# Prefetching transfers moved from SyncE's queue to ScalarE's, and parts of the next chunk's preparation moved forward, in a fused mLSTM and FFN kernel

## The chip, the cores and the metric

The kernel runs on one core of one Trainium2 chip. The metric is device time in microseconds (us); the runs of one kernel lay 0.15 to 1.4% apart. The compute engines are TensorE (PE; PEld is its weight load), VectorE (DVE), ScalarE (ACT) and GpSimd (POOL). SyncE (SP) only issues transfers in this kernel. "SPq" and "ACTq" are the transfers issued from SyncE's and ScalarE's instruction streams.

## The reference

Two blocks follow each other: an mLSTM cell over 4 batches, 8 heads, 768 steps and head size 40, then a squared-ReLU FFN from 320 to 2048 and back on the 3072 tokens.

```python
for t in range(S):                                   # mLSTM, per batch and head
    m_new = maximum(f[t] + m, i[t])
    C = exp(f[t] + m - m_new) * C + exp(i[t] - m_new) * outer(v[t], k[t])
    n = exp(f[t] + m - m_new) * n + exp(i[t] - m_new) * k[t]
    y[t] = sigmoid(o_gate[t]) * (C @ q[t]) / maximum(abs(n @ q[t]), 1)
x = y, heads side by side                            # 3072 x 320
h = maximum(x @ w_in, 0)
return (h * h) @ w_out
```

## The kernel before

The steps are cut into 24 chunks of 128 steps; the attention is computed chunk by chunk, with a state C carried from one to the next. TensorE's attention work of a chunk stands between parts of the FFN of earlier chunks, so that TensorE always has something to do. The main loop has four FFN parts a chunk (`at` is 0 to 3) and starts with chunk 6.

Turning matrices is done without TensorE: data goes out to DRAM and comes back in a layout in which VectorE's 32x32 transposes finish the turn. So a chunk needs many small transfers: k and q out ("pair-ups", four, `kq_rows`) and in ("squares", four, `kqT`), the numerator out and back (`num_rows`), x out and back (`x_rows`, `xT`), and a broadcast of decay rows (`A_bc`). All of them are issued by SyncE, in program order.

```python
def pair_up(s):                      # four transfers, k and q of chunk s
    ...
            nc.sync.dma_start(kq_d[s, i, n]..., src[b, ...]...)

def load_squares(s):                 # four transfers
    ...
            nc.sync.dma_start(t[...], kq_d[s, i, ...]...)

def score(s):
    scores(s)                        # k q^T on TensorE
    weighted(s)                      # P = scores * W, on VectorE
    scale_q(s)                       # q's product: decay times turned q, on VectorE

for n, (which, g, i) in enumerate(parts):
    s, at = 6 + n // 4, n % 4
    ...
    if at == 0:
        do(score, s)
    if at == 1:
        do(attend_turned, s)         # numT = C q + V P on TensorE, then tn (a transpose) and the new C
        ...
    if at == 3:
        do(normalise_turned, s)      # x from num and the gate, on VectorE
        do(store_rows, s)            # x out and back, five transfers
        if s % 4 == 3:               # chunks 7, 11, 15, 19
            ... sigmoid(r) ...       # the gates of four later chunks, on ScalarE
    ... the FFN part: matmuls, ReLU on ScalarE, squares on VectorE, or the copy of m1 on ScalarE ...
    if at == 2:
        do(load_squares, s + 2)
        do(weigh_on, s + 1)          # W on ScalarE, then the broadcast load_A(s + 3)
        do(turn_kq, s + 1)
    if at == 3:
        do(decay_C, s + 1)
    ...
    if at == 1:
        do(move_num, s)              # num out and back, five transfers
        do(load, s + 4)
        do(pair_up, s + 3)
```

The second half of the FFN uses a Strassen-like scheme: the first product of a step is copied by ScalarE (`m1`, the row `y_sb<-h_ps` of the ACT timeline), and the copy has to be done before TensorE may reuse its PSUM bank.

## Time and profile before

| | before |
|---|---|
| time, median of 3 | 541.83 us (541.43 to 542.83) |
| span of the profiled run | 542.6 us |
| TensorE busy / idle | 525.0 / 17.6 us |
| mean granted TensorE clock | 0.987 |
| ScalarE busy | 193.5 us (36%) |
| median from issue to landing of x's store | 4.2 us |

The prediction shows the lines on TensorE. In the view of waits, a row names engine, tile and line, what released it, then total us, times, and longest:

```profile
ACT r_sb L647 <- PE h_ps L632: 151.9, 24, 10.4
...
ACT y_sb L740 <- PE h_ps L715: 66.8, 11, 7.5
...
ACT y_sb L735 <- PE h_ps L715: 54.7, 11, 10.6
```

ScalarE waits for TensorE.

### The profile page before, as it was taken

Reading aid. Unit: us, or ns where it says so; the run is one execution under the profiler, and the core shown is the slowest. Engines: PE = TensorE matmul, PEld = TensorE weight load, DVE = VectorE, ACT = ScalarE, POOL = GpSimd, SP = SyncE. Lnnn points to the kernel's source line nnn. Section 1 sums busy time; section 2 is a strip of 40 time slices with the busy share of each in tenths; the row PEclk is TensorE's granted clock in tenths of the full one; section 3 lists DMA queues with packets and bytes.
Section 4 is the critical chain, followed back from the end, with each engine's and each line's share of the span. In section 5 each row is a group of like instructions: output and inputs, shape, how many; then the busy total and the mean of one; then the engine's idle time right before and its main releaser. Section 6 shows DMA issues by size and latency. Waiting matters only on the chain.

```text
span 542.6 us, 10288 instructions
## 1 busy us (share of the span) xinstructions
PE 525.0 (97%) x3929; PEld 457.9 (84%) x3929; DVE 333.0 (61%) x620; ACT 193.5 (36%) x460; POOL 97.1 (18%) x110
## 2 busy tenths in 40 slices
PE   9989989997999989999999999999999999999997
PEld 4868878885788988888888898888898888898997
DVE  8488988866865664565575575465575485341631
ACT  3767576470531431522422533321433413101100
POOL 3355633321211320011210111000111010000000
PEclk9897999998999999999999999999999999999999
DMA  9988698847557747657657557568555241120000
GB/s 192 227 186 198 151 175 196 207 127 137 119 134 138 143 115 148 130 131 148 129 127 153 129 124 157 122 131 158 128 124 125 61 94 44 40 53 1 26 24 25
DMA packets 238353, 67.53 MB, mean 124 GB/s; under 512 B 185728, under 2 KB 232832, under 8 KB 238304
## 3 DMA queue, kind: packets, MB, share of 16 engines
q1 hardware_dynamic: 238208, 66.68, 57.5%
q8 instruction: 31, 0.51, 0.4%
q10 hardware_dynamic: 96, 0.20, 0.1%
q14 instruction: 18, 0.15, 0.1%
HBM read 54.56 MB, written 17.86 MB: 133 GB/s over the span
## 4 chain that ended last, share of the span: by engine, by line
PE 74%; DVE 10%; DMA 7%; SPq 4%; issue 2%; ACT 2%; POOL 0%; DVEq 0%; POOLq 0%; ACTq 0%
PE h_ps L621 26%; PE h_ps L715 25%; PE h_ps L632 7%; PE tp L422 3%; PE numT L512 3%; PE numT L505 3%; PE h_ps L661 3%; DMA x_rows<-x_sb 2%; DMA xT<-x_rows 2%; PE hp L458 1%; DVE g L654 1%; DMA num_rows<-tn 1%; SPq L308 1%; ACT W_sb L384 1%; DMA raw<-in_moe_w_out_dram 1%
## 5 line engine op out<-in xcount | busy, mean ns | idle before, releaser
L621 PE MATMUL h_ps<-xT,w_in 128*128 128x256 f32 x768 | 175.8, 384 | 3.8 <-DVE xT L597 2.8
L621 PEld LDWEIGHTS h_ps<-xT,w_in 128*128 128x128 f32 x768 | 143.7, 191 | 26.5 <-DVE xT L597 4.2
L647 ACT ACTIVATE r_sb<-h_ps 128x512 f32<-128x512 f32 x96 | 50.0, 601 | 155.0 <-PE h_ps L632 151.9
L654 DVE TENSOR_TENSOR g<-r_sb 128x512 f32<-128x512 f32 x96 | 61.7, 702 | 60.8 <-ACT r_sb L647 60.8
L715 PE MATMUL h_ps<-w_out,g 128*128 128x160 f32 x528 | 77.0, 302 | 0.0
L715 PEld LDWEIGHTS h_ps<-w_out,g 128*128 128x128 f32 x528 | 72.5, 190 | 1.4
L358 POOL TENSOR_SCALAR_AFFINE_SELECT A_bc<-A_bc 128x1024 f32<-128x1024 f32 x22 | 27.2, 1237 | 200.5 <-ACT kq L368 105.5
L384 ACT ACTIVATE W_sb<-A_bc,b_T 128x128 f32<-128x128 f32 x176 | 53.8, 391 | 24.3 <-POOL A_bc L358 24.2
L715 PE MATMUL h_ps<-T,S 128*128 128x160 f32 x352 | 52.3, 302 | 0.0
L715 PEld LDWEIGHTS h_ps<-T,S 128*128 128x128 f32 x352 | 48.8, 190 | 3.0 <-ACT r_sb L647 3.0
L632 PE MATMUL h_ps<-xT,w_in 64*128 64x256 f32 x384 | 49.0, 391 | 0.0
L632 PEld LDWEIGHTS h_ps<-xT,w_in 64*128 64x128 f32 x384 | 34.8, 186 | 12.3 <-issue 9.0
L597 DVE STREAM_TRANSPOSE xT<-xT 128x384 f32<-128x384 f32 x18 | 10.4, 576 | 46.3 <-DMA xT<-x_rows 46.3
L396 POOL TENSOR_TENSOR vw<-va,W_sb 128x328 f32<-128x328 f32 x20 | 20.1, 1003 | 86.6 <-ACT W_sb L384 74.9
L731 DVE TENSOR_TENSOR y_sb<-y_sb,h_ps 128x160 f32<-128x160 f32 x44 | 14.1, 320 | 33.8 <-PE h_ps L715 32.6
L435 DVE TENSOR_TENSOR P_sb<-tp,W_sb 128x512 f32<-128x512 f32 x46 | 29.5, 683 | 1.9 <-PE tp L422 1.9
L527 DVE STREAM_TRANSPOSE tn<-numT 128x512 f32<-128x512 f32 x18 | 12.9, 717 | 28.0 <-PE numT L512 28.0
L740 ACT COPY y_sb<-h_ps 128x160 f32<-128x160 f32 x11 | 3.2, 293 | 66.8 <-PE h_ps L715 66.8
L422 PEld LDWEIGHTS tp<-kqT 40*128 40x128 f32 x384 | 24.2, 187 | 3.3 <-issue 2.3
L422 PE MATMUL tp<-kqT 40*128 40x128 f32 x384 | 26.9, 279 | 0.0
L715 PE MATMUL h_ps<-T,g 128*128 128x160 f32 x176 | 25.7, 299 | 0.0
L715 PE MATMUL h_ps<-w_out,S 128*128 128x160 f32 x176 | 25.7, 299 | 0.0
(119 smaller groups left out, 626.6 us busy)
## 6 DMA issues: line engine op xcount, KB each, us to landing
A_bc<-a_rows SPq DMA_DIRECT2D x22, 512.0 KB, 5.0
raw<-in_moe_w_out_dram SPq DMA_DIRECT2D x16, 320.0 KB, 3.4
num_rows<-tn SPq DMA_DIRECT2D x18, 256.0 KB, 2.3
kq<-num_rows SPq DMA_DIRECT2D x72, 64.0 KB, 1.9
kqT<-kq_rows SPq DMA_DIRECT2D x34, 128.0 KB, 2.9
raw<-in_moe_w_in_dram SPq DMA_DIRECT2D x8, 512.0 KB, 4.8
kq<-in_k_dram SPq DMA_DIRECT2D x24, 160.0 KB, 3.4
va<-in_v_dram SPq DMA_DIRECT2D x24, 160.0 KB, 3.9
```

The source lines that it names most:

```text
L358: nc.gpsimd.affine_select(A[:], A[:], compare_op=ALU.is_ge, fill=-1e30, base=0, pattern=[[0, H], [1, P]], channel_multiplier=-1,)
L384: nc.scalar.activation(d["W"][:, i * n + h, :], A[i][:, h, :], AF.Exp, bias=b_T[:, b, c, i * n + h : i * n + h + 1],)
L396: nc.gpsimd.tensor_tensor(d["vw"][:], d["va"][:], d["W"][:, :, P - 1 : P].to_broadcast([P, H, D1]), op=ALU.mult,)
L422: nc.tensor.matmul(sc[i][:, j, :], lhsT=d["kT"][rows, j, :], rhs=d["qT"][rows, j, :], start=True, stop=True,)
L435: nc.vector.tensor_tensor(t, d["sc"][i], d["W"][:, heads, :], op=ALU.mult)
L505: nc.tensor.matmul(numT[halves[i], j, :], lhsT=C[live[i], j * D1 : j * D1 + DP], rhs=d["eA"][live[i], j, :], start=(j == 0), stop=False, s ...
L512: nc.tensor.matmul(numT[halves[i], j, :], lhsT=va_w[s % NKQ][:, h * D1 : h * D1 + DP], rhs=d["P"][h % 2][:, h // 2, :] if s < KQ_SQ else d ...
L621: nc.tensor.matmul(hs[i][:, n, :], lhsT=w_in[:, a, fb * P : (fb + 1) * P], rhs=xT[:, :, a, :], start=(n == 0 and a == 0), stop=False,)
L632: nc.tensor.matmul(hs[i][:, n, :], lhsT=w_in2[rows, 2 * pp + n, :], rhs=xT[rows, :, 2, :], start=False, stop=(n == 1),)
L647: nc.scalar.activation(rs[-1][:], h[:], AF.Relu)
L654: nc.vector.tensor_tensor(g4[:, :, i, :], r[:], r[:], op=ALU.mult)
L715: nc.tensor.matmul(to, lhsT=lhsT[:, p], rhs=rhs[:, p, :], start=(start and p == 0), stop=(p == NPAIR - 1), skip_group_check=True,)
```

## The change

Its intent: free SyncE for the transfers that the current chunk's result hangs on (num, x and the output), and have decays, mask, turn and q's product of the next chunk ready one or two FFN parts earlier.

```diff
-    def pair_up(s):
+    def pair_up(s, queue):
...
-                nc.sync.dma_start(
+                queue.dma_start(
... (the same in load_squares and load_A)
     def score(s):
         scores(s)
         weighted(s)
-        scale_q(s)
...
         if at == 1:
             do(attend_turned, s)
+            do(decays, s + 1)
+            do(mask, s + 1)
+            if n > 4:
+                do(turn_kq, s + 1)
+            do(decay_C, s + 1)
...
+        if at == 2:
+            do(lambda s: load_squares(s, nc.scalar), s + 2)
+            if n > 4:
+                do(scale_q, s + 1)
         if at == 3:
-            do(normalise_turned, s)
-            do(store_rows, s)
+            do(lambda s: pair_up(s, nc.scalar), s + 3)
             ... (sigmoids, then the FFN part)
         if at == 2:
-            do(load_squares, s + 2)
-            do(weigh_on, s + 1)
-            do(turn_kq, s + 1)
-        if at == 3:
-            do(decay_C, s + 1)
+            do(lambda s: weigh(s, masked=True), s + 1)
+            do(lambda s: load_A(s, nc.scalar), s + 2)
+            if n < 4:
+                do(turn_kq, s + 1)
+                do(scale_q, s + 1)
+            do(normalise_turned, s)
+            do(store_rows, s)
...
         if at == 1:
             do(move_num, s)
             do(load, s + 4)
-            do(pair_up, s + 3)
```

Cut here: one of the two S sums of the FFN moves as well, and the broadcast is loaded two chunks ahead, not three.

## The prediction

> **What bounds the kernel now.** I read the page first, then the waits of TensorE, then its timeline for every gap, and last the timelines of the queues that the change touches. From the page, engine busy time and the chain of waits by engine:
>
> ```profile
> PE 525.0 (97%) x3929; PEld 457.9 (84%) x3929; DVE 333.0 (61%) x620; ACT 193.5 (36%) x460; POOL 97.1 (18%) x110
> PE 74%; DVE 10%; DMA 7%; SPq 4%; issue 2%; ACT 2%; POOL 0%; DVEq 0%; POOLq 0%; ACTq 0%
> ```
>
> TensorE works 525.0 of 542.6 us. Its instructions are the same, in the same order, in both built kernels, so only its idle time, 542.6 - 525.0 = 17.6 us, can change. The waits of TensorE say who ends it (total us, times, longest):
>
> ```profile
> PE numT L505 <- DVE kq L483: 6.3, 6, 2.9
> PE h_ps L621 <- DVE xT L597: 2.8, 3, 1.1
> PE h_ps L621 <- DMA num_rows<-tn: 0.4, 1, 0.4
> ```
>
> These three are the ones in the loop that the change edits, which starts near 103 us. The timeline of TensorE gives the gaps one by one (start, duration, instructions; idle before in brackets):
>
> ```profile
> 128.87 1.09 PE L505 MATMUL numT<-kq,C 40*64 40x128 f32 x16 [2.91 <-DVE kq L483]
> ...
> 276.23 1.09 PE L505 MATMUL numT<-kq,C 40*64 40x128 f32 x16 [0.64 <-DVE kq L483]
> ...
> 365.00 7.17 PE L621 MATMUL h_ps<-xT,w_in 128*128 128x256 f32 x32 [1.12 <-DVE xT L597]
> ```
>
> Waits for q's product (numT, L505): 2.91 once, then 0.64, 0.64, 0.65, 0.65, 0.85. Waits for the turned x (L621): 0.37, 0.83, 0.88, 1.12. Sum 2.91 + 3.43 + 3.20 = 9.5 us. The other gaps lie before 100 us, in code that does not change. So the floor is 541.8 - 9.5 = 532.3 us, 1.8% faster: a gain of over 2% is not there to be had.
>
> Why x is late shows in SP's timeline around one chunk (queue start, time in issue):
>
> ```profile
> 265.77 1.45 SPq L286 DMA_DIRECT2D kq_rows<-in_k_dram  x2
> 267.27 1.83 SPq L286 DMA_DIRECT2D kq_rows<-in_q_dram  x2
> 269.19 0.53 SPq L749 DMA_DIRECT2D out_dram<-y_sb  x1
> 269.77 2.67 SPq L308 DMA_DIRECT2D kqT<-kq_rows  x4
> 272.54 0.59 SPq L333 DMA_DIRECT2D A_bc<-a_rows  x1
> 274.09 0.38 SPq L588 DMA_DIRECT2D x_rows<-x_sb  x1
> 278.10 1.86 SPq L590 DMA_DIRECT2D xT<-x_rows  x4
> ```
>
> The prefetches (4 pair-ups, 4 squares, 1 broadcast) take 1.45 + 1.83 + 2.67 + 0.59 = 6.5 us of SP in a chunk of 20.5 us, and stand just ahead of x. And x's store needs 4.0 us to land, behind the broadcast. Sizes and median time from issue to landing, from the page:
>
> ```profile
> A_bc<-a_rows SPq DMA_DIRECT2D x22, 512.0 KB, 5.0
> x_rows<-x_sb SPq DMA_DIRECT2D x18, 192.0 KB, 4.2
> xT<-x_rows SPq DMA_DIRECT2D x72, 48.0 KB, 2.3
> ```
>
> Late in the run, with little else in flight, x's store lands in 2.1 us (438.90 to 440.99), so about half of the 4.2 is queueing.
>
> **What the Trainium skill says.** "DMA: Bandwidth & Descriptors", Issuing engines are not separate DMA queues: transfers started by ScalarE run on the same 16 DMA engines; a second issuer saves only sequencer time. The trace allows that: moving issue frees SP by 6.5 us a chunk, but not the DMA engines, busy about 65% in mid-run. "Perfetto Trace Analysis", DMA Instruction - HWDGE: the recorded window of an issue ends when the sequencer is free, without the data movement; here 0.38 us for x against 4.0 us to land. So the 6.5 us of issue are what ScalarE takes over. "ScalarE: Activation LUTs", What ACT_TABLE_LOAD costs: about 1283 ns a load; the trace shows 1.28 us.
>
> **The change, part by part.**
>
> (1) q's product (0.68 us on VectorE) goes from behind P to the chunk before. In the gap at 276.23, P ends at 275.4 and q's product at 276.0, and numT needs q first. Afterwards numT starts on q, done long before, and reaches P one microsecond later. The five small gaps go: -3.43 us.
>
> (2) x's normalisation no longer stands behind the turn of k and q (1.24 us) and the second S sum (1.65 us); the product ahead of it adds 0.68. With the store no longer behind prefetches, x starts some 4 us earlier in odd chunks (270.1 for 274.1) and over 6 us earlier in even ones (287 for 293.52). The four gaps are at most 1.12 us: -3.20 us.
>
> (3) ScalarE now issues nine transfers a chunk, and each can block it. The built program hands out eight DMA semaphores in rotation; each issue waits until the transfer that last used its semaphore has landed. I followed every one. In steady chunks ScalarE's last pair-up waits for a first or second piece of the same chunk's xT, on SP's queue: for tn, num out and back, normalisation, x out and xT in. Behind that stand ReLU in even chunks, and sigmoids and the copy of m1 in odd ones. ScalarE inherits x's latency.
>
> Sigmoid chunks (11, 15, 19). ScalarE before:
>
> ```profile
> 310.71 1.28 ACT L326 ACT_TABLE_LOAD   x1
> 312.01 1.55 ACT L326 ACTIVATE og<-og 128x320 f32<-128x320 f32 x4
> 314.89 0.29 ACT L735 COPY y_sb<-h_ps 128x160 f32<-128x160 f32 x1 [1.34 <-PE h_ps L715]
> ```
>
> TensorE needs that copy at 320.10 - 0.65 = 319.45. Afterwards: x normalised 311.6, store landed 313.8 to 315.5, second xT issued 0.5 later and landed 2.0 to 2.3 later, 316.3 to 318.3; issue 0.6, table 1.28, sigmoids 1.55, copy 0.29: 320.0 to 322.0. Stall 0.6 to 2.6, estimated low, 0.9, since x should queue less: 3 x 0.9 = +2.7 us.
>
> Even chunks. tn ends 278.4, num lands after 2.3, its return takes 1.75 to issue and 1.9 to land, normalisation 2.05, store 2.3 to 3.9, xT 2.1 to 2.4, issue 0.6: ReLU starts between 291.4 and 293.4 (before: 291.43). ReLU's first tile 0.6, four squares 2.5, P 1.2: P is ready 295.7 to 297.7, wanted at about 297.1. Mostly hidden: eight chunks at 0.1, +0.8 us.
>
> The first chunk of the loop. Now:
>
> ```profile
> 119.72 2.07 ACT L647 ACTIVATE r_sb<-h_ps 128x512 f32<-128x512 f32 x4 [0.19 <-PE h_ps L632]
> ```
>
> Afterwards the squares, P's exponentials, the broadcast, two pieces of weight rounding and four pair-ups stand ahead of it, and the third pair-up waits for x's store of chunk 6. Its num lands at 122.5 in the trace, so x starts at 124.4, lands 126.5 at the earliest, two issues: ReLU from 127.7 at the earliest, squares to 130.8, P to 132.0. numT has q at once and reaches P at 127.0: 5.0 us idle where 2.91 are now, +2.1. The fourth pair-up waits for the broadcast, issued near 125; at its median of 5.0 ReLU starts near 130.6 and the loss is +5. I take +3.0 us net.
>
> Sum: 541.8 - 3.4 - 3.2 + 2.7 + 0.8 + 3.0 = 541.7. The stalls are upper-heavy but the order of work looks worked over by hand, which makes me lean to the low ends: **541.0 us**.
>
> **The rivals.** A: the intended gain, ScalarE's spare time swallows the issues. For: it is 36% busy, its time before ReLU in the chunk at 291.43 is idle 5.3 us. Against: the semaphore waits are not in busy time. It makes 535 to 537. B: ScalarE becomes the path; every even chunk loses about 1 us, sigmoid chunks 2.5, the start 6. For: the loop from tn through ReLU to the next tn comes to about 20 us, TensorE's own period 20.45. Against: x should land in nearer 2.3 than 4.2 us when it is not queued behind the broadcast. It makes 541.8 - 6.6 + 8 + 7.5 + 6 = 557 at worst, 548 if half of that. C: the gaps of x were hidden by DMA traffic that stays the same: x still lands in 4.2 us, and only (1) counts. Against: its start moves by 4 us where 1.12 was missing. With the same ScalarE costs it makes 545.
>
> **Range and chances.** The point lies between A and half of B. Range 534 to 549. Faster by over 2% would need 531.0, under the floor: 0.02. Slower by over 2% needs 552.7, rival B nearly whole: 0.06. Within 2%: 0.92.
>
> **What would show it.** Right: no wait of numT on q's product, none of L621 on xT except near zero; SP's x store 4 us earlier in its chunk; new gaps of TensorE before the first L715 of a step after a sigmoid, released by ScalarE's copy; near 127 us a gap before L512 (numT from P), longer than 2.91, with ReLU behind ScalarE's issues. Wrong: if ScalarE's issues end well before ReLU and copies are due, rival A holds; if P is waited for in every even chunk, B; if the changed kernel takes over 549 I have undervalued x's latency, and under 534 I have missed a cost of TensorE itself.

## The result, and the profile after

The changed kernel took **569.89 us** (568.82 to 572.88, 4 runs), against 542.33 (541.43 to 544.8, 4 runs) for the kernel before. The ratio is **1.0509**, 95% interval 1.0453 to 1.0566. A ratio is the mean time of one kernel's runs over that of the other's of the same rounds, so it isn't quite the ratio of the medians. The predicted 541.0 and the range to 549 were missed.

The page after, engine busy time and the chain of waits by engine:

```profile
PE 534.3 (94%) x3928; PEld 463.6 (81%) x3929; DVE 329.4 (58%) x620; ACT 192.9 (34%) x460; POOL 92.1 (16%) x110
PE 46%; DMA 27%; DVE 13%; ACT 5%; SPq 5%; issue 3%; ACTq 2%; POOL 0%; DVEq 0%; POOLq 0%
```

The span is 571.1 us, 28.5 more. TensorE's idle time is 571.1 - 534.3 = 36.8 us, 19.2 more, and its busy time 9.3 more for the same work. The chain now runs through transfers for 27% of the span (7% before). ScalarE is *less* busy than before: time stood at an issue isn't counted as busy.

TensorE's waits in the loop:

```profile
PE h_ps L713 <- ACT y_sb L733: 11.0, 6, 4.0
PE numT L510 <- DVE P_sb L433: 8.3, 6, 7.4
PE h_ps L619 <- ACT r_sb L645: 8.1, 6, 1.9
```

The waits for q's product and for the turned x, 9.5 us before, are gone, as planned. Three new ones of 27.4 us stand in their place. The timeline of TensorE, one example or more of each (start, duration, instructions; idle before in brackets):

```profile
136.57 2.35 PE L510 MATMUL numT<-P_sb,va 128*64 128x128 f32 x15 [7.44 <-DVE P_sb L433]
...
206.28 4.61 PE L713 MATMUL h_ps<-w_out,g 128*128 128x160 f32 x32 [0.86 <-ACT y_sb L733]
224.43 2.78 PE L619 MATMUL h_ps<-xT,w_in 128*128 128x256 f32 x8 [1.89 <-ACT r_sb L645]
253.38 5.99 PE L713 MATMUL h_ps<-w_out,g 128*128 128x160 f32 x32 [4.02 <-ACT y_sb L733]
...
314.98 1.99 PE L619 MATMUL h_ps<-xT,w_in 128*128 128x256 f32 x8 [1.19 <-ACT r_sb L645]
...
429.68 6.29 PE L713 MATMUL h_ps<-w_out,g 128*128 128x160 f32 x32 [3.10 <-ACT y_sb L733]
```

From the whole timeline: 7.44 in the first chunk; the copy behind the sigmoids of chunks 11, 15 and 19 4.02 + 1.65 + 3.10 = 8.8; behind those of chunk 7, which the prediction left out, 1.12 (at 162.16); the copy in odd chunks without sigmoids (9 and 17) 0.86 + 0.24 = 1.1; ReLU in even chunks six gaps, 8.1. Note that the 32 matmuls of L713 take 4.61 us after a short gap and 5.99 or 6.29 after a long one; more on that below.

What ScalarE waits for now:

```profile
ACT r_sb L645 <- PE h_ps L630: 107.7, 16, 10.0
ACT r_sb L645 <- DMA kq_rows<-in_k_dram: 34.1, 5, 7.6
ACT W_sb L382 <- DMA kq<-num_rows: 32.2, 7, 6.3
...
ACT r_sb L645 <- DMA kq_rows<-in_q_dram: 16.1, 2, 8.9
...
ACT L326 <- DMA xT<-x_rows: 14.8, 2, 8.0
```

ReLU waits for TensorE 16 times where it was 24; in seven others of this list it waits for a transfer named `kq_rows`, a pair-up. ReLU reads nothing of that; it stands behind it in ScalarE's instruction stream. The last row is the sigmoids' table load (L326), which twice waited, by the profile, for x's return, xT, of which it reads nothing either. ScalarE's and SyncE's timelines around the sigmoids of chunk 11 show how:

```profile
242.60 1.21 ACTq L286 DMA_DIRECT2D kq_rows<-in_k_dram  x2
249.07 1.21 ACTq L286 DMA_DIRECT2D kq_rows<-in_q_dram  x2
250.31 1.28 ACT L326 ACT_TABLE_LOAD   x1 [7.91 <-issue]
251.60 1.55 ACT L326 ACTIVATE og<-og 128x320 f32<-128x320 f32 x4
253.06 0.27 ACT L733 COPY y_sb<-h_ps 128x160 f32<-128x160 f32 x1
```

```profile
242.31 0.37 SPq L586 DMA_DIRECT2D x_rows<-x_sb  x1
246.18 2.73 SPq L588 DMA_DIRECT2D xT<-x_rows  x4
```

Two pair-ups are issued by 243.8. By the waits in the built program, the next can't be until x has gone out (242.31, landed near 246.1, when its return is issued) and a piece of xT has come back, near 249. ScalarE stands there for 5.3 us, then needs 1.28 for the table and 1.55 for the sigmoids, and only then does the copy run at 253.06, for which TensorE has been idle for 4.02 us.

### The profile page after: what moved, and what is told of

Same layout as the page of the kernel before. It is cut to its first block, busy times and chain, and to the rows that moved or that the text cites. A ratio compares the mean times of both kernels' runs of the same rounds, so it can differ in the third digit from the quotient of the medians.

```text
span 571.1 us, 10291 instructions
## 1 busy us (share of the span) xinstructions
PE 534.3 (94%) x3928; PEld 463.6 (81%) x3929; DVE 329.4 (58%) x620; ACT 192.9 (34%) x460; POOL 92.1 (16%) x110
## 4 chain that ended last, share of the span: by engine, by line
PE 46%; DMA 27%; DVE 13%; ACT 5%; SPq 5%; issue 3%; ACTq 2%; POOL 0%; DVEq 0%; POOLq 0%
PE h_ps L713 17%; PE h_ps L619 13%; DMA x_rows<-x_sb 10%; DMA num_rows<-tn 5%; PE h_ps L630 4%; DMA kq<-num_rows 4%; DMA xT<-x_rows 3%; DVE g L652 3%; DMA kqT<-kq_rows 2%; PE numT L510 2%; SPq L539 2%; PE hp L456 2%; PE tp L420 2%; ACTq L286 2%; DVE P_sb L433 1%
## 5 line engine op out<-in xcount | busy, mean ns | idle before, releaser
L619 PE MATMUL h_ps<-xT,w_in 128*128 128x256 f32 x768 | 180.3, 390 | 8.7 <-ACT r_sb L645 8.1
L619 PEld LDWEIGHTS h_ps<-xT,w_in 128*128 128x128 f32 x768 | 145.7, 194 | 33.1 <-ACT r_sb L645 10.5
L713 PE MATMUL h_ps<-w_out,g 128*128 128x160 f32 x528 | 80.0, 310 | 11.0 <-ACT y_sb L733 11.0
L713 PEld LDWEIGHTS h_ps<-w_out,g 128*128 128x128 f32 x528 | 75.5, 196 | 12.8 <-ACT y_sb L733 11.7
L382 ACT ACTIVATE W_sb<-A_bc,b_T 128x128 f32<-128x128 f32 x176 | 53.8, 388 | 64.5 <-DMA kq<-num_rows 32.2
L713 PE MATMUL h_ps<-T,S 128*128 128x160 f32 x352 | 52.3, 302 | 0.0
L713 PEld LDWEIGHTS h_ps<-T,S 128*128 128x128 f32 x352 | 48.8, 190 | 3.0 <-ACT r_sb L645 3.0
L358 POOL TENSOR_SCALAR_AFFINE_SELECT A_bc<-A_bc 128x1024 f32<-128x1024 f32 x22 | 24.3, 1103 | 148.3 <-ACT kq L368 124.9
L510 PE MATMUL numT<-P_sb,va 128*64 128x128 f32 x288 | 23.3, 288 | 8.9 <-DVE P_sb L433 8.3
L729 DVE TENSOR_TENSOR y_sb<-h_ps,y_sb 128x160 f32<-128x160 f32 x11 | 3.6, 325 | 45.1 <-ACT y_sb L733 35.4
L510 PEld LDWEIGHTS numT<-P_sb,va 128*64 128x64 f32 x288 | 17.3, 141 | 14.2 <-DVE P_sb L433 11.8
L713 PE MATMUL h_ps<-w_out,S 128*128 128x160 f32 x176 | 25.7, 299 | 0.0
L713 PE MATMUL h_ps<-T,g 128*128 128x160 f32 x176 | 25.7, 299 | 0.0
```

Of the source, the lines that this page charges most:

```text
L358: nc.gpsimd.affine_select(A[:], A[:], compare_op=ALU.is_ge, fill=-1e30, base=0, pattern=[[0, H], [1, P]], channel_multiplier=-1,)
L382: nc.scalar.activation(d["W"][:, i * n + h, :], A[i][:, h, :], AF.Exp, bias=b_T[:, b, c, i * n + h : i * n + h + 1],)
L510: nc.tensor.matmul(numT[halves[i], j, :], lhsT=va_w[s % NKQ][:, h * D1 : h * D1 + DP], rhs=d["P"][h % 2][:, h // 2, :] if s < KQ_SQ else d ...
L619: nc.tensor.matmul(hs[i][:, n, :], lhsT=w_in[:, a, fb * P : (fb + 1) * P], rhs=xT[:, :, a, :], start=(n == 0 and a == 0), stop=False,)
L713: nc.tensor.matmul(to, lhsT=lhsT[:, p], rhs=rhs[:, p, :], start=(start and p == 0), stop=(p == NPAIR - 1), skip_group_check=True,)
L729: add = lambda to, a, b: nc.vector.tensor_tensor(to, a, b, op=ALU.add)
```

## The experiments

Three theories were set against each other. **W**: ScalarE stands at issues that wait for earlier transfers to land, and what stands behind them is late. **I**: the issue time itself, nine a chunk, is too much for ScalarE. **M**: the moves of turns, masks and q's product do the harm. Diffs are against the changed kernel unless said.

### Where the transfers are issued

**all_sp**: the three prefetches back to SyncE, all moves kept.

```diff
-            do(lambda s: load_squares(s, nc.scalar), s + 2)
+            do(lambda s: load_squares(s, nc.sync), s + 2)
... (the same for pair_up and load_A)
```

> The changed kernel with its three prefetches (pair-ups, squares, broadcast) issued by SP again, order of work otherwise as changed. Theory W (ScalarE stands at issues that wait for landings of SP's transfers) and theory I (issuing costs ScalarE too much time by itself) both expect 534 to 542 us, with no wait of TensorE on ReLU or on the copy of m1. Theory M (the moved turns, masks and product are what costs) expects 560 us or more.

547.98 us, ratio 1.0103 (1.0063 to 1.0144). Of a loss of 5%, 1% is left, so most of it comes from ScalarE's queue. But the expected gain did not come: with all issues on SyncE the moves alone cost 1.0% (0.6 to 1.4%). TensorE's waits and, below, SyncE's timeline:

```profile
PE h_ps L619 <- DVE xT L595: 6.8, 5, 2.5
PE numT L510 <- DVE P_sb L433: 4.1, 1, 4.1
```

```profile
355.32 3.32 SPq L308 DMA_DIRECT2D kqT<-kq_rows  x4
358.73 0.68 SPq L749 DMA_DIRECT2D out_dram<-y_sb  x1
359.52 0.38 SPq L333 DMA_DIRECT2D A_bc<-a_rows  x1
359.99 0.62 SPq L586 DMA_DIRECT2D x_rows<-x_sb  x1
```

x is normalised by 356.65 but sits behind squares, an output store and the broadcast until 359.99. My expectation had left out SyncE's queue, which is as long as before: x, ready earlier, waits 3.3 us in it.

**queues_only**: the kernel *before*, with only the three prefetches on ScalarE, nothing moved.

```diff
-                nc.sync.dma_start(          # in pair_up, load_squares and the loop's load_A
+                queue.dma_start(            # queue = nc.scalar in the loop
```

> The kernel before with only the three prefetches moved to ScalarE's queue, its order of work kept. There pair-ups come before x's store in the order in which semaphores are handed out, so they wait for num's return and not for x. W expects 541 to 553 us: waits shorter by the x store and xT (about 6 us a chunk) than in the changed kernel. I expects the whole loss, 565 us or more, since ScalarE issues the same nine transfers a chunk. M expects about 542.

615.5 us, ratio 1.1324 (1.1277 to 1.1370), clock 0.941. The queue alone does harm, and more than the whole change. That rules out M as the cause of the loss, since it expected 542, but not I, which expected 565 or more: W's size (553 at most) was far off, and the other runs have to part W from I. TensorE's waits, then ScalarE's timeline of one chunk:

```profile
PE numT L505 <- DVE kq L483: 26.8, 13, 11.5
PE h_ps L621 <- ACT r_sb L647: 26.6, 7, 5.7
```

```profile
318.36 2.78 ACTq L286 DMA_DIRECT2D kq_rows<-in_q_dram  x2
321.27 5.54 ACTq L308 DMA_DIRECT2D kqT<-kq_rows  x4
326.86 1.27 ACT L368 ACTIVATE kq<-A_bc 64x512 f32<-64x512 f32 x2 [9.46 <-DMA x_rows<-x_sb]
329.32 2.45 ACT L384 ACTIVATE W_sb<-A_bc,b_T 128x128 f32<-128x128 f32 x8 [1.20 <-POOL A_bc L358]
...
332.23 2.06 ACT L647 ACTIVATE r_sb<-h_ps 128x512 f32<-128x512 f32 x4 [0.46 <-ACT W_sb L384]
```

Here the squares stand directly behind the pair-ups, decays (L368), mask and W behind the squares, and ReLU last. All these times are in series, and by the profile the 9.46 us end with x's store, which my expectation had excluded. In the changed kernel these pieces stand apart, and the loss is 28 us for 73. So the moves together soften the harm of ScalarE's issuing, the opposite of M; which of them does was not run.

**pair_sp**: only the four pair-ups back to SyncE.

```diff
-            do(lambda s: pair_up(s, nc.scalar), s + 3)
+            do(lambda s: pair_up(s, nc.sync), s + 3)
```

> The changed kernel with only the pair-ups back on SP; squares and broadcast stay on ScalarE. W expects 534 to 545 us, because only the pair-ups wait for x and xT. I expects about 5/9 of the loss over the all-SP version to stay, some 555 us. M expects 565 or more.

539.08 us, ratio 0.9930 (0.9897 to 0.9963). One line turns a loss of 5% into a gain of 0.7%. Its only wait in the loop is 5.7 us for P in the first chunk. The squares on ScalarE still wait, up to 7.9 us, but mostly with nothing due behind them.

**pair_early**: the same nine issues on ScalarE, pair-ups one part earlier, ahead of the squares.

```diff
         if at == 2:
+            do(lambda s: pair_up(s, nc.scalar), s + 3)
             do(lambda s: load_squares(s, nc.scalar), s + 2)
...
         if at == 3:
-            do(lambda s: pair_up(s, nc.scalar), s + 3)
```

> The changed kernel with the pair-ups still on ScalarE but emitted ahead of the squares, thus ahead of x's store in the hand-out of semaphores: the same nine issues a chunk, none waiting for x or xT, only for num's return. W expects most of the loss gone, 536 to 550 us. I and M expect 565 or more.

551.29 us, ratio 1.0150 (1.0116 to 1.0184): just above W's range, far from what I and M expect. TensorE's waits for ReLU are down to 0.4 us and those for the copy to 4.4; the first chunk's gap, 7.7, stays.

**store_after**: x's store emitted after the pair-ups, to give the semaphores to other transfers.

```diff
         if at == 3:
             do(lambda s: pair_up(s, nc.scalar), s + 3)
+            do(store_rows, s)
...
-            do(store_rows, s)            # at the end of at == 2
```

> The changed kernel with one call moved: x's store and its return are emitted just after the pair-ups, in place of just before. Instruction order on ScalarE and on SP stays exactly the same; only which transfer last held the semaphore of each pair-up changes (squares, broadcast, gate and value loads, no longer x and xT). W expects most of the 28 us gone: 540 to 552 us, gaps before ReLU and the copy of m1 under 0.5 us each in steady chunks. I (issue time) expects 565 or more.

568.14 us, ratio 1.0463 (1.0442 to 1.0484). W's 540 to 552 was missed, but the run was no test of it. The pair-ups still waited for pieces of the same chunk's xT, because semaphores are handed out in the scheduled order, not in the order of the source. In effect the changed kernel ran a second time.

**pair_last**: the pair-ups with the very same waits, placed behind the FFN part of their step.

```diff
         if at == 3:
-            do(lambda s: pair_up(s, nc.scalar), s + 3)
             ... sigmoids, FFN part ...
+        if at == 3:
+            do(lambda s: pair_up(s, nc.scalar), s + 3)
```

> The changed kernel with ScalarE's four pair-ups placed behind that step's FFN part, so behind the ReLU, the sigmoids and the copies of the step, not ahead of them. The waits of the pair-ups in the built program were compared one by one before the run: they are the same transfers as in the changed kernel, pieces of the same chunk's xT among them. W (ScalarE stands at issues that wait for landings, and what stands behind them is late): the waits of TensorE for ReLU (8.1 us) and for the sigmoid chunks' copy (most of 11.0 us) go, the first chunk stays near 8 us; 538 to 550. I (nine issues take ScalarE's time wherever they stand): 560 or more. M (the moves themselves harm): 568 as the changed kernel.

541.33 us, ratio 0.9981 (0.9947 to 1.0014). TensorE's waits:

```profile
PE numT L510 <- DVE P_sb L433: 5.0, 1, 5.0
PE h_ps L713 <- ACT y_sb L733: 2.3, 2, 1.5
```

```profile
233.76 2.58 ACTq L286 DMA_DIRECT2D kq_rows<-in_k_dram  x2
237.03 1.21 ACTq L286 DMA_DIRECT2D kq_rows<-in_q_dram  x2
238.28 0.29 ACT L733 COPY y_sb<-h_ps 128x160 f32<-128x160 f32 x1 [5.27 <-DMA kq_rows<-in_k_dram]
```

The eight microseconds for ReLU are gone and 2.3 of 11.0 are left for the copy. ScalarE issues the same nine transfers, four of them with the same waits, in another place: 28.6 us less (569.89 to 541.33, a ratio to the kernel before of 0.9981 where it was 1.0509). x's store takes 3.8 us in the median in both, so it isn't that x landed sooner. ScalarE still stands at its issues, up to 7.8 us before a copy. In chunk 11 the copy even stays behind the pair-ups (second fence: ScalarE's timeline); what went ahead of them there is the table and the sigmoids, 2.83 us. This is the clearest run for W: ScalarE has the time, and what matters is the order in its stream.

### The first chunk, and the moves

**first_sp**: chunk 6 alone put back (squares and pair-ups on SyncE, x one part later).

```diff
-            do(lambda s: load_squares(s, nc.scalar), s + 2)
+            do(lambda s: load_squares(s, nc.sync if n < 4 else nc.scalar), s + 2)
-            do(lambda s: pair_up(s, nc.scalar), s + 3)
+            do(lambda s: pair_up(s, nc.sync if n < 4 else nc.scalar), s + 3)
... (normalise_turned and store_rows at at == 3, ahead of pair_up, for n < 4)
```

> The changed kernel with chunk 6 alone (the first of the loop) put back: its squares and pair-ups on SyncE and its normalisation and x store one part later, all other chunks as in the changed kernel. It parts the loss by place. W: only the gap of 7.4 us before numT's second half goes, down to 3 or less, with the slow matmuls behind it (1 to 3 us): 560 to 565. A rival that puts the loss into the start of the loop alone: 545 or less. A rival in which the start costs nothing, because the lost time is given back later: 567 to 570.

560.51 us, ratio 1.0331 (1.0281 to 1.0381). The gap shrinks from 7.44 to 2.20, and about 9 us of the loss are gone; the remaining 18 lie in the later chunks. The six runs spread from 556.29 to 564.30, and the profile is of the slowest.

**best**: first_sp and pair_sp together.

```diff
-            do(lambda s: load_squares(s, nc.scalar), s + 2)
+            do(lambda s: load_squares(s, nc.sync if n < 4 else nc.scalar), s + 2)
-            do(lambda s: pair_up(s, nc.scalar), s + 3)
+            do(lambda s: pair_up(s, nc.sync), s + 3)
... (normalise_turned and store_rows as in first_sp)
```

> Pair-ups on SP as in the version that beat the kernel before, and for the loop's first chunk also the squares on SP and the normalisation behind the weight rounding as before the change. The 5.7 us gap before numT's second half near 130 us should shrink to 1 to 2 us and the slow matmuls after it go: 532 to 536 us. If that gap comes from elsewhere it stays near 539.

535.15 us, ratio 0.9854 (0.9832 to 0.9876). It beats both kernels; one gap of 2.4 us is left in the loop.

**scale_back**: pair_sp with q's product back behind P.

```diff
     def score(s):
         scores(s)
         weighted(s)
+        scale_q(s)
... (scale_q removed at at == 2)
```

> Pair-ups on SP, and only q's product put back behind P of its own chunk. My step (1) expects its five gaps of 0.64 to 0.85 back: +3.4 us over the pair-ups-on-SP version, some 542.5, with waits of numT on q's product. A rival: with VectorE freed earlier in the chunk the product is no longer late, and the time stays near 539.

541.44 us, ratio 0.9982 (0.9964 to 0.9999), 2.4 over pair_sp's 539.08, some 2.8 by the ratios. The sum is near what was expected, but it came from elsewhere. TensorE's waits:

```profile
PE numT L503 <- DVE kq L481: 8.4, 2, 7.9
```

The first chunk's gap is 7.9 for 5.7; of the five small gaps in steady chunks only one came back, with 0.5. The rest of the change, with SyncE free and x normalised earlier on VectorE, already brings P and q's product in time. Which part of it does so was not run.

**turn_back**: pair_sp with turn and q's product both back ahead of the normalisation.

```diff
-            if n > 4:
-                do(turn_kq, s + 1)       # at at == 1
-            if n > 4:
-                do(scale_q, s + 1)       # at at == 2
...
-            if n < 4:
-                do(turn_kq, s + 1)
-                do(scale_q, s + 1)
+            do(turn_kq, s + 1)
+            do(scale_q, s + 1)
```

> Pair-ups on SP, and the turn of k and q plus q's product put back ahead of x's normalisation in the same part. If the turn's place on VectorE was what made x late, waits for xT of 0.4 to 1.1 us return, +2 to +3 us (541 to 542). If it was SP's queue, the time stays near 539.

538.28 us, ratio 0.9923 (0.9898 to 0.9948): the same as pair_sp. So the turn's place on VectorE, with q's product ahead of the normalisation too, is worth nothing that these runs can measure.

### Why the same matmuls took longer

The stretches of the changed kernel after its 7.44 us gap; columns: stretch, length, busy time of PE, PEld, DVE, ACT and POOL, granted clock, DMA share, GB/s.

```profile
136.50:139.00 2.50, 2.43 (x23) 2.10 (x25) 1.66 (x5) 0.00 (x0) 0.62 (x1) 0.50 0.00 0
139.00:145.00 6.00, 6.00 (x32) 4.45 (x31) 5.75 (x8) 0.43 (x1) 1.74 (x3) 0.90 0.01 3
145.00:152.00 7.00, 7.00 (x27) 4.94 (x27) 3.03 (x4) 2.44 (x8) 0.14 (x1) 1.00 0.72 147
```

TensorE comes back from the gap at half its clock. The Trainium skill, "TensorE: Matmul & The Clock Gate", Part 1, says just this: after an idle window of about 3.4 us the clock is halved until about 3.4 us of sustained work. The trace agrees with the 0.50, and by these rows the half clock lasted until about 140.2, an estimated 3.6 us after TensorE came back at 136.57. Theory **C** says that idleness causes it.

**clock_fill**: pair_sp, with 24 matmuls on zeros in its gap of 5.7 us.

```diff
+        if s == 7:                       # between the two halves of numT
+            t = ps_at.tile([P, W], F32, name="fill", tag="at")
+            for _ in range(24):
+                nc.tensor.matmul(t[:], lhsT=zeros..., rhs=zeros..., start=True, stop=True)
```

> The kernel pair_sp (539.08) with 24 matmuls on zeros put into its one gap of 5.7 us, between the two halves of numT of chunk 7; nothing reads them. C (idleness of TensorE lowers its granted clock for some us afterwards): the 15 matmuls of numT's second half take about 1.1 us for 2.36, the granted clock of the 7.6 us behind the gap is over 0.9 for 0.65, and the time is 1.5 to 3 us less than pair_sp of the same rounds. Rival (the matmuls behind the gap are slow for another reason: their operands, the transfers beside them, the order of P's halves): the same 2.36 us, and the time within 1 us of pair_sp.

543.03 us, ratio 1.0007 (0.9979 to 1.0035). Both expectations fell: the filling matmuls wrote a bank that was free only once P was done, so they waited through the gap and then came on top. The run was still useful: the fill itself ran slowly, and behind it numT's 16 matmuls took 1.09 us, at full speed. So the operands of numT aren't what is slow.

```profile
131.06 0.58 PE L510 MATMUL fill<-zeros 128*128 128x512 bf16 x1 [5.62 <-DVE P_sb L433]
131.87 7.02 PE L510 MATMUL fill<-zeros 128*128 128x512 bf16 x22 [0.22 <-issue]
138.82 1.09 PE L516 MATMUL numT<-P_sb,va 128*64 128x128 f32 x16
```

**pair_sp_again**: pair_sp without any edit, for comparison in the same rounds.

> The same kernel as pair_sp, for comparison with clock_fill in the same rounds: ratio 0.990 to 0.996 as before, with the gap near 5.7 us and the clock behind it near 0.65.

538.14 us, ratio 0.9929 (0.9890 to 0.9967), as before; gap 5.92.

**fill_early**: the same fill in a bank that is free before the gap.

```diff
-            t = ps_at.tile([P, W], F32, name="fill", tag="at")
+            t = ps_h.tile([P, W], F32, name="fill", tag="h_ps")
```

> As clock_fill (pair_sp with 24 matmuls on zeros between the two halves of numT of chunk 7), but in a PSUM bank whose last reader is done before the gap: in the built program the first of them waits only for a step of ScalarE at 126 us, before the gap begins. C (idleness of TensorE lowers its granted clock for some us afterwards): the gap is filled, the matmuls of numT's second half take 1.0 to 1.1 us for 2.35, the flow behind it runs at a granted clock over 0.9, and the time is 1.5 to 3 us less than pair_sp (ratio 0.987 to 0.991 for 0.993). Rival (another reason than idleness): the 2.35 us stay, ratio 0.992 or more.

535.67 us, ratio 0.9863 (0.9831 to 0.9895). By the ratios that is 3.6 us less than pair_sp_again, more than C's 1.5 to 3; the two ran in different rounds, and their intervals just touch. The mean granted clock of the profiled run is 1.000, in part by luck: it kept the full clock near 41 us too, where pair_sp_again lost it. The other five runs have 0.987 to 0.994, those of pair_sp_again 0.980 to 0.986. First pair_sp_again's timeline, then this one's:

```profile
131.00 2.35 PE L510 MATMUL numT<-P_sb,va 128*64 128x128 f32 x15 [5.92 <-DVE P_sb L433]
...
134.04 14.59 PE L659 MATMUL h_ps<-w_out,g 128*128 128x320 f32 x48
```

```profile
124.73 5.42 PE L510 MATMUL fill<-zeros 128*128 128x512 bf16 x23
...
130.72 0.98 PE L516 MATMUL numT<-P_sb,va 128*64 128x128 f32 x13 [0.16 <-DVE P_sb L433]
...
132.04 13.19 PE L665 MATMUL h_ps<-w_out,g 128*128 128x320 f32 x48
```

P comes no sooner than before but for 0.3 us (130.72 for 131.00), yet what follows runs 1.4 us faster in the 48 matmuls, and about one in numT. So the idleness of the gap is the cause of the slow matmuls behind it.

**best_fill**: best with ten such matmuls in its gap of 2.4 us.

```diff
+        if s == 7:                       # added to best, between the two halves of numT
+            t = ps_h.tile([P, W], F32, name="fill", tag="h_ps")
+            for _ in range(10):
+                nc.tensor.matmul(t[:], lhsT=zeros..., rhs=zeros..., start=True, stop=True)
```

> The kernel best (535.15, ratio 0.9854) with 10 matmuls on zeros in its one gap of 2.4 us. C (even 2.4 us of idleness lowers the granted clock afterwards): the 13 matmuls of numT's second half take 0.98 us for 1.76, the 48 matmuls behind them 13.19 for 13.65, the granted clock of the 8 us behind the gap is over 0.95, and the time is 0.8 to 1.5 us less than best (ratio 0.982 to 0.985). Rival (a gap of 2.4 us is too short, the slowness behind it has another reason): 1.76 and 13.65 stay, ratio 0.985 or more.

532.50 us, ratio 0.9798 (0.9754 to 0.9843). The timeline of best, then this one's:

```profile
130.43 13.65 PE L659 MATMUL h_ps<-w_out,g 128*128 128x320 f32 x48
```

```profile
127.48 1.09 PE L516 MATMUL numT<-P_sb,va 128*64 128x128 f32 x16
...
128.81 13.19 PE L665 MATMUL h_ps<-w_out,g 128*128 128x320 f32 x48
```

The 48 matmuls end at 142.0 for 144.1, and the clock there is 1.00 (0.66 and 0.86 in best). So 2.4 us of idleness were enough. By the medians the gain is 2.7 us, more than C's 0.8 to 1.5, but the two ran in different rounds and their intervals overlap a little, so its size is loose; whether the whole is over 2% faster than the kernel before stays open. This is the fastest kernel.

The kept traces say more on which gaps count. The clock stands at 1.00 or 0.50 and changes in steps of 3.41 us (0.50 from 130.40 to 133.81 in the kernel before, from 225.49 to 228.90 in the changed one). Counted on this grid over all kept traces from 95 to 510 us, 33 of 34 falls to 0.50 come behind a step in which TensorE idled 1.87 us or more (the other: 1.58), and no step that left the clock at 1.00 had over 1.75. So what seems to count is how much of one step a gap fills. This is a count and no experiment, and before 95 us the clock also fell behind steps with 0 to 1.7 us of idleness, so there is another cause as well.

## Why the prediction was wrong

**The gains, steps (1) and (2): the waits went, the sizes were not additive.** All waits for q's product and for xT went. But scale_back shows that four of step (1)'s five small gaps (3.43 us) go by the rest of the change alone, if the pair-ups stay on SyncE; moving q's product was worth 0.5 in steady chunks and 2.2 in the first. And all_sp shows that step (2) hangs on SyncE being free: with the queue as long as before, the waits for xT were 6.8 us, where the kernel before had 3.2. In the changed kernel x does start as early as step (2) reckoned: in one even chunk 11.3 us behind numT (306.49 - 295.18) for 17.3 (293.52 - 276.23).

**The costs, step (3): right mechanism, terms mis-sized.** "ScalarE inherits x's latency" is what happened, in the three places named. The sum of +6.5 us was the failure:

| term | predicted | measured |
|---|---|---|
| sigmoid chunks 11, 15, 19 | +2.7 | +8.8 |
| sigmoid chunk 7 | 0 | +1.1 |
| odd chunks without sigmoids | 0 | +1.1 |
| even chunks | +0.8 | +8.1 for ReLU, +0.9 for P |
| first chunk | +3.0 | 7.4 - 2.9 = +4.5 |
| TensorE's busy time | 0 | +9.3 |

The measured idle terms come to 24.5 us. Less the 6.6 of (1) and (2) that is +17.9 in the loop; with 1.3 more of idleness, the rest, it is the 19.2, and with the 9.3 the 28.5 us between the two profiled runs. Two steps failed in the idle terms.

The first is "x should queue less". x's store still took 3.8 us in the median, and 5.4 in one even chunk (306.49 to 311.86), where 2.2 to 3.9 was reckoned with. In chunk 11 from x's issue to the second pair of pair-ups it is 249.07 - 242.31 = 6.8 us, just past the upper end of my own working (4.7 to 6.7), and I took the low end. The upper end would have given a stall of 2.6; most of the rest of the 4.02 are two issues behind the landing where I had one (1.21 us for 0.6), and an x that left 0.8 us nearer to the time at which the copy was due. Why x's store stayed slow can be seen though no run isolates it: the 512 KB broadcast is now issued from the other queue at 241.16, 1.2 us ahead of x. Taking it off SyncE did not take it out of x's way. Other chunks fit: in the loop of the changed kernel x's return is issued 3.3 to 5.7 us after x where the broadcast went out under 2 us ahead, and in that of pair_sp 2.1 to 4.2 where it went out 2.4 us or more ahead. The Trainium skill's "DMA: Bandwidth & Descriptors", Issuing engines are not separate DMA queues, which I had quoted, says that the engines are shared; I applied it to bandwidth and not to this pair.

The second is "Mostly hidden" for even chunks. I asked only when P would be late. In the trace TensorE stops earlier, at a matmul of L619 that needs the PSUM bank that a late ReLU has not yet read: 1.19 us at 314.98, with only 0.17 left to wait for P. I had followed the data and not the buffer.

Also missed was that the squares wait too, for num's return (32.2 us of ScalarE's waits); in the first chunk they held it 6.7 us, and ReLU started at 132.66 where I had put 127.7 to 130.6.

**The premise "only its idle time ... can change" fell.** Busy time grew by 9.3 us, a third of the loss. Of these, 1.5 lie ahead of the loop (97.4 us for 95.9 up to the same matmuls, which start at 103.05 after and 100.90 before) and are not the change's. About 5 lie behind the new gaps: in the stretches at clock 0.50 (133.3 to 140.2, 225.5 to 228.9, 252.8 to 256.2 and 430.3 to 433.7 us) TensorE was busy 13.2 us, half of which is lost, 6.6 us, against 1.7 in the one stretch of the kernel before. That idleness does this, fill_early and best_fill show for two gaps. The other 3 us or so are spread over the loop, and their cause stays open. The trace of before had the slow clock already: behind its 2.91 us gap it was 0.73 and 0.70 for six microseconds, hidden in a 20 us stretch that I read as 0.91. So the floor of 532.3 us was no floor, since 525.0 us of busy time contained slow matmuls: best_fill's profiled span, 530.3 us, is under 542.6 - 9.5 = 533.1, though its median, 532.50, is at the floor and not clearly below.

**The rivals.** B was right in kind ("ScalarE becomes the path"); its 557 "at worst" was still 13 us short, mainly for the 9.3. (The "548 if half of that" is a slip: half of its costs makes 541.8 - 6.6 + 10.75 = 546.) A fell for the place of the issues, not for ScalarE's capacity: pair_last has them all and takes 541.33.

## What to carry to other kernels

Before an issue of a transfer is put on an engine that computes, list what its wait is for and what stands behind it in that engine's stream; the engine's busy share did not show it here (36% before, 34% after), and moving four issues behind the urgent work took back the whole loss. A late ReLU or copy holds a PSUM bank, so follow buffers as well as data. Expect a gap of TensorE of some 2 us or more to cost more than its length, and look at the granted clock in stretches of a few microseconds behind it.

## What the Trainium skill lacked or had wrong

- "DMA: Bandwidth & Descriptors", Issuing engines are not separate DMA queues: the section says that a second issuer saves sequencer time, and names no cost to that issuer. Here ScalarE stood 5.3 us in one pair of issues (243.8 to 249.07), and the place of four issues in its stream was worth 28.6 us (569.89 against 541.33).
- No page has it: a transfer's issue can wait for an unrelated one to land, because a program hands out few semaphores in rotation (eight here). 50.2 us of ReLU's waiting (34.1 + 16.1) ended at such pair-ups, and TensorE lost 8.1 us by it.
- "TensorE: Matmul & The Clock Gate", HAM oscillation: it gives idle gaps over about 3.4 us as the ones to avoid. Here 2.4 us lowered the clock (0.66 and 0.86 behind it in best), and filling that gap gave 532.50 for 535.15 us. Gaps of 1.89 us (224.43, eight matmuls in 2.78 us) were followed by slow matmuls too, while others of about the same size were not (1.69 us at 401.18, the eight matmuls in 1.99). On the grid of 3.41 us steps the first idled 1.89 us of one step and the second 1.61. The halved clock itself, 0.50, is as the page has it.
